# RWKV-5 attention and soft-MoE slots on one core: one key half moved to GpSimd's load queue, a three-row last weight piece, and a new order

## The chip, the core and the metric

The kernel runs on one core of a Trainium2 chip. A core has five engines that run side by side and meet through semaphores: TensorE (PE in the profile; its weight loads stand apart as PEld), VectorE (DVE), ScalarE (ACT), GpSimd (POOL) and SyncE (SP). Transfers between the chip's main memory and the on-chip memory run on sixteen DMA engines. They are issued from SP's, ScalarE's or GpSimd's queue; only GpSimd's can turn fp32 into bf16 on the way. The metric is the device time of one execution in microseconds (us).

## The reference

Two parts, one behind the other. First a linear attention over 768 steps, for 4 batches and 8 heads of width 48, with a decaying 48 by 48 state for each head; then a mixture of experts, in which 32 slots (8 experts of 4) take softmax-weighted means of all 3072 tokens, go through a two-layer network each, and are mixed back to the tokens.

```python
for t in range(S):
    kt, vt, rt = (k[:, :, t], v[:, :, t], r[:, :, t])
    cur = np.einsum('bhd,bhe->bhde', u[None] * kt, vt)
    y[:, :, t] = np.einsum('bhd,bhde->bhe', rt, state + cur)
    state = w[None, :, :, None] * state + np.einsum('bhd,bhe->bhde', kt, vt)
...
x = np.ascontiguousarray(attn_out.transpose(0, 2, 1, 3)).reshape(B * S, H * D)
logits = x @ phi
d = softmax over the tokens, c = softmax over the slots
slot_input = d.T @ x
h = np.maximum(slot_input[e] @ w1[e], 0.0)
slot_out[e] = h @ w2[e]
return c @ slot_out
```

All inputs and the output are fp32. k, r and v have 1.18 million elements each, phi is 384 by 32, w1 is 8 by 384 by 1024, w2 8 by 1024 by 384, the output 3072 by 384.

## The kernel before

**Loads.** The 768 steps are cut into six chunks of 128. Each chunk of k, r and v comes in two halves (two batches each, 192 KB as bf16): L0 and L1 are the halves of k for chunk 0, L2 and L3 those of r, L4 and L5 those of v, and so on up to L35. Behind them on the same queue come the eight w1 (W0 to W7, 768 KB each) and the eight w2 (V0 to V6, and expert 7 in two pieces, Va7 with its first rows and Vb7 with the last YL rows; a row is 1/8 of an expert's w2, 96 KB). All of these are issued by GpSimd, which converts them to bf16, except L0 and L1: these are loaded as fp32 into `k0`, a corner of the w1 buffer that is still free, L0 by SP and L1 by ScalarE (lines 253 and 254). phi and u are loaded by SP behind L0, w by ScalarE ahead of L1. GpSimd's issue waits until one of the last eight loads has landed, so that at most eight of its loads are in flight. w2 goes into the buffers of the chunks of k, r and v, so its issue also waits for the copies out of them (line 822).

**Set-up.** DVE clears and fills constants; GpSimd makes an index table and the identity, and clears the padding of the two rp buffers (line 267). `zt0` to `zt3` (DVE) and `ze0` to `ze3` (ACT) make the tables of decay factors, `za`, `zb`, `zd` the mask, the u column and phi in bf16. `fill(n)` issues n dummy products on PE.

**A chunk.** `q..` copies a loaded tensor with padding into an rp buffer (for chunk 0 of k in two halves, `qk00` and `qk01`); `t..` turns it with 16 transposes on PE (line 376), `e..` takes it out of PSUM on DVE or ACT, for k and r with the decay factors. `A` and `M` are the scores and their mask, `pr`, `D`, `ds` and `dv` the diagonal term, `b` and `kn`, `vn` the transposes back, `s` and `S` the state, `Y` and `x` the output of the attention, `X`, `xT`, `l` and `lg` the logits. `mx`, `sb`, `ex`, `c` and `cT` make the weights of the slots for the way back. After chunks 3, 5 and 6 a group (`gm` to `acc`) adds the tokens' share to the slots' inputs with a running maximum.

**The end.** `h` is the first expert layer (48 products), `hs` its relu, `ht` and `hT` its transpose. `o00` to `o70` are the second layer, expert by expert, eight rows each, in one PSUM bank SO. For expert 7 the work is cut: `o70` takes the rows of Va7, then `so1` copies the sum so far; `o7` with the remaining rows (`o76` for rows 6 and 7) completes it and `so2` copies that. The first four of the 24 output rows (128 tokens each) do not wait for so2: their product `p` uses so1, and the last weight rows are added from `gG`, a product of the hidden layer with cT that is made earlier, one for each of these rows (`pg`, line 795, YL products for each output row; row 0 is made in halves a and b). The other 20 use so2. `oe` takes a row out of PSUM, even rows on ACT, odd ones on DVE, and `dm` (SP) stores one, two, four or eight rows. The order around it is fixed by `turn_`: p0a, p0b, p1, pg0a, pg0b, pg1, the last o, p2, pg2, p3, pg3, p4.

**The order.** The order in which all of this is issued, on every engine, is written out by hand in the string `ORDER`. A token is a piece's name; the numbers behind the colon are its buffers, a letter behind a slash its engine (D, A or P). `WARM` lists dummy products `F0`, `F1`, ... on PE and the piece each batch stands behind: three behind o50, six behind o60, three behind o70.

Of the kernel before, what the change touches and what calls it, by code (L numbers as in the profile page):

```python
# [21 lines left out]
A000:0,0 pr00:0/D tk10:1,1 ev01:/A iL16 M000 tk11:2 pr01:/P kn00:/A bk01:3,1 bv00:4,0 ek10 A001:0,1 ek11 vn00:/A  # L22
bv01:5,1 iL17 qr1:0/D D0:0,0 qv1:1/A s00:1,2,0 M001 iL18 tr10:4,1 iL19 S101 ds0:/A vn01:/A A010:0,2 iL20 tr11:0
S100 iL21 bk10:2,2 er10 qk2:0/A bk11:5,0 iL22 er11 tv10:1,1 dv00:0 M010 tv11:4 kn10:/A qr2:1/A ev11:/D iL23
Y000:0,0 kn01:/D Y001:2 iL24 A011:0,0 iL25 s01:4,3,1 x000:/A M011 x001:/A tk20:0,0 iL26 ev10:/A X00:2,0 pr10:0/P
S111 A100:0,1 kn11:/A tk21:1 ek20 tr20:3,0 xT00:/A M100 bv10:5,2 qv2:0/A bv11:0,3 iL27 tr21:2 ek21 iL28 pr11:/D
bk20:1,1 iL29 vn10:/A er21 iL30 kn20:/A er20 s10:5,2,2 iL31 vn11:/A qk3:1/D tv20:1,0 iL32 S110 bk21:3,2 dv01:1 S200
D1:0,1 kn21:/A ev20:/D s11:4,5,3 S201 ds1:/A tv21:1 iL33 pr20:0/D Y011:3 iL34 ev21:/A Y010:0,1 S210 A101:0,0 iL35
pr21:/D l00:2 x010:/A bv20:4,0 iW0 M101 x011:/A D2:1,0 dv10:0 bv21:0,1 vn20:/A X01:3,1 lg00:/D ds2:/A A110:0,2 S211
# [76 lines left out]
def kernel(  # L106
# [13 lines left out]
    B, H, S, D = r.shape  # L120
# [34 lines left out]
    pe, dve, act, pool, sp = nc.tensor, nc.vector, nc.scalar, nc.gpsimd, nc.sync  # L155
# [12 lines left out]
    def raw_t(x):  # L168
        return raw[:, x * RAWN:(x + 1) * RAWN]
# [60 lines left out]
    def load_rkv(y):  # L230
        x, bb = divmod(y, 2)
        c, which = divmod(x, 3)
        src = (k, r, v)[which].rearrange("(bb bl) h (c p j) d -> c bb (bl h) p (j d)", bb=2, bl=2, p=RR, j=JJ)
        O(pool.dma_start(out=raw_t(x)[:, bb * JJ * D:(bb + 1) * JJ * D], in_=src[c, bb]))  # L234
# [8 lines left out]
    def fill(n):  # L243
        for _ in range(n):
            O(pe.matmul(pG[0][:], ones[:, 0:128], ones[:], start=True, stop=True))

    P.fill = fill
    k0 = early[:, 2560:2560 + 2 * JJ * D]


    k_src = k.rearrange("(bb bl) h (c p j) d -> c bb (bl h) p (j d)", bb=2, bl=2, p=RR, j=JJ)
    O(act.dma_start(out=w_r[:, :, 0:D], in_=w[:, None, :].to_broadcast([H, 2, D])))
    for bb, q in ((0, sp), (1, act)):
        O(q.dma_start(out=k0[:, bb * JJ * D:(bb + 1) * JJ * D], in_=k_src[0, bb]))
    O(act.preload_act_table_set("natural_log_exp_and_others"))
    O(dve.memset(ident_f[:], 0.0))
    for t in (w_r, u_r):
        O(dve.memset(t[:, :, D:], 1.0))
    O(dve.memset(ones[:], 1.0))
    O(sp.dma_start(out=phi_f[:], in_=moe_phi.rearrange("(p mo) s -> p mo s", mo=nM)))  # L260
    O(sp.dma_start(out=u_r[:, :, 0:D], in_=u[:, None, :].to_broadcast([H, 2, D])))
    O(pool.iota(it_i.rearrange("p (j y) -> p j y", j=JJ), pattern=[[-1, JJ], [-JJ, RR]], base=C - 1,
                channel_multiplier=0))
    O(pool.affine_select(out=ident_f[:], in_=ident_f[:], compare_op=ALU.not_equal, fill=1.0, base=0,
                         pattern=[[-1, 128]], channel_multiplier=1))
    for t in rp_r:
        O(pool.memset(t[:, :, :, D:], 0.0))
# [85 lines left out]
    def turn(c, which):  # L353
# [506 lines left out]
```

## Time and profile before

| | |
|---|---|
| time, median of 3 runs | 117.49 us (117.24 to 117.93) |
| time of the profiled execution | 117.38 us |
| its span, first to last instruction | 115.6 us |
| PE busy | 98.7 us, 85% |
| PE weight loads | 76.0 us, 66% |
| DVE busy | 89.8 us, 78% |
| ACT busy | 76.7 us, 66% |
| POOL busy | 66.4 us, 57% |
| GpSimd's DMA queue (q0) | 19.27 MB, 85.7% of the sixteen engines' span |
| SP's DMA queue (q1) | 5.16 MB, 11.8% |
| ScalarE's DMA queue (q10) | 0.40 MB, 1.4% |
| read and written in main memory | 39.38 MB, 4.72 MB |

A row of the timeline or of a group reads: start, time, engine, line of the kernel, operation, what is written and read, shape, count, and in brackets how long the engine stood idle before and for whom. A row "DMA to landing" is the time from the start of an issue to the last of its sixteen completions. A row of the chain of waits is start, time, engine, what is written and the line. A row of a table by stretch is the stretch, its length, the busy time of PE, PEld, DVE, ACT and POOL with counts, the granted clock, the DMA engines' share and GB/s. A row of a DMA queue in a stretch is its number and kind, packets, MB, and the time its packets took as a share of sixteen engines; packets overlap, so that this can pass 100%.

### The profile page before, as it was taken

How to read it: one execution, taken by the hardware profiler on the slowest of the kernel's cores; microseconds unless marked ns; L12 is line 12 of the kernel's file. 1: busy time of each engine (PE TensorE's matmuls, PEld its weight loads, DVE VectorE, ACT ScalarE, POOL GpSimd, SP SyncE). 2: the span in 40 equal slices, each digit the busy share in tenths (PEclk: the TensorE clock that was granted, in tenths of full speed). 3: DMA queues.
4: the chain of work that ended last, by engine and by line, in shares of the span. 5: the costliest groups of instructions: out<-in, count | busy, mean ns of one | idle time of the engine just before them, and what ended most of it. 6: DMA issues, size and time to landing. Idle time of an engine off the chain costs nothing.

```text
span 115.6 us, 3911 instructions
## 1 busy us (share of the span) xinstructions
PE 98.7 (85%) x1649; PEld 76.0 (66%) x1649; DVE 89.8 (78%) x178; ACT 76.7 (66%) x124; POOL 66.4 (57%) x85
## 2 busy tenths in 40 slices
PE   4906999989899999999989999999999999999000
PEld 0306998869788889888868898888664653453000
DVE  6745979999999989999999999999883730379400
ACT  2947088999879797979996662898853440189100
POOL 7925589999699998069999999656030000000000
PEclk9999999999999999999999999999999999999965
DMA  2999999999999999999999999999999997059994
GB/s 36 268 197 206 207 205 210 205 206 208 208 210 201 229 219 208 218 219 212 210 220 215 210 220 210 214 219 212 215 223 208 217 209 149 17 208 404 408 438 174
DMA packets 9137, 25.08 MB, mean 217 GB/s; under 512 B 1184, under 2 KB 6176, under 8 KB 8992
## 3 DMA queue, kind: packets, MB, share of 16 engines
q0 software_dynamic: 7344, 19.27, 85.7%
q1 hardware_dynamic: 1608, 5.16, 11.8%
q10 hardware_dynamic: 168, 0.40, 1.4%
q8 instruction: 13, 0.21, 0.7%
q14 instruction: 4, 0.03, 0.1%
HBM read 39.38 MB, written 4.72 MB: 381 GB/s over the span
## 4 chain that ended last, share of the span: by engine, by line
PE 48%; DMA 17%; DVE 11%; ACT 9%; POOL 5%; issue 3%; DVEq 0%; ACTq 0%; POOLq 0%
DMA w_all<-in_moe_w_dram 17%; PE pG L376 9%; PE pA L415 4%; PE pG L788 3%; ACT rp L222 3%; PE pG L397 3%; PE pA L826 3%; PE pG L743 3%; PE pG L633 2%; PE pG L716 2%; PE pG L516 2%; PE pG L551 2%; POOL w_all L237 2%; PE pG L490 2%; PE pG L496 2%
## 5 line engine op out<-in xcount | busy, mean ns | idle before, releaser
L421 DVE TENSOR_TENSOR AT<-pA,mask 128x1024 bf16<-128x1024 f32 x24 | 29.2, 1218 | 1.3 <-PE pA L415 1.1
L376 PE MATMUL pG<-ident,rp 128*128 128x128 bf16 x288 | 22.5, 235 | 2.6 <-DVE rp L224 2.4
L376 PEld LDWEIGHTS <-rp 128*128 128x128 bf16 x288 | 19.2, 106 | 3.8 <-issue 2.8
L428 POOL TENSOR_TENSOR pr<-kT,rT 128x1024 bf16<-128x1024 bf16 x8 | 17.0, 2130 | 5.1 <-DVE rT L386 4.6
L445 POOL TENSOR_TENSOR dv<-vn,ds 128x768 bf16<-128x768 bf16 x12 | 17.7, 1482 | 3.0 <-DVE sd L540 2.2
L222 ACT COPY rp<-raw 128x1536 bf16<-128x1536 bf16 x11 | 16.3, 1479 | 2.6 <-PE pG L376 2.3
L222 ACT COPY vT<-pG 128x1024 bf16<-128x1024 bf16 x8 | 8.0, 1015 | 5.2 <-PE pG L376 5.2
L474 DVE TENSOR_TENSOR S<-pG,W 128x384 bf16<-128x384 f32 x20 | 10.5, 548 | 0.5 <-PE pG L466 0.5
L803 ACT ACTIVATE w_all<-pG,rcs 128x384 f32<-128x384 f32 (+1 forms) x12 | 5.8, 587 | 6.1 <-PE pG L795 5.9
L415 PE MATMUL pA<-rT,kT 64*128 64x128 bf16 x192 | 9.5, 218 | 0.3 <-DVE AT L421 0.2
L386 DVE TENSOR_TENSOR kT<-pG,Tk 128x1024 bf16<-128x1024 bf16 x12 | 8.0, 684 | 1.7 <-PE pG L376 1.3
L222 ACT CAST x<-pG 128x384 bf16<-128x384 f32 x19 | 8.5, 487 | 0.8 <-PE pG L498 0.5
L222 ACT COPY xT<-pG 128x768 bf16<-128x768 bf16 x10 | 8.0, 804 | 1.3 <-PE pG L516 1.2
L496 PE MATMUL pG<-vn,AT 128*128 128x48 bf16 x192 | 8.7, 183 | 0.2 <-ACT kn L222 0.2
L222 ACT COPY vn<-pG 128x768 bf16<-128x768 bf16 x10 | 8.0, 815 | 0.9 <-PE pG L397 0.9
L805 DVE TENSOR_SCALAR w_all<-pG,rcs 128x384 f32<-128x384 f32 (+1 forms) x13 | 6.9, 596 | 1.6 <-PE pG L795 1.6
L234 POOL DMA_DIRECT2D raw<-in_v_dram x12 | 6.3, 537 | 3.1 <-DMA raw<-in_r_dram 3.0
L386 DVE TENSOR_TENSOR rT<-pG,Tr 128x1024 bf16<-128x1024 bf16 x12 | 7.9, 683 | 0.0
L498 PE MATMUL pG<-dv,ident 128*128 128x384 bf16 x24 | 7.7, 323 | 0.0
L222 ACT COPY kn<-pG 128x768 bf16<-128x768 bf16 x9 | 7.3, 812 | 0.5 <-PE pG L397 0.5
L415 PEld LDWEIGHTS <-kT 64*128 64x128 bf16 x192 | 5.7, 94 | 2.8 <-issue 1.1
L496 PEld LDWEIGHTS <-AT 128*128 128x128 bf16 x192 | 7.1, 96 | 0.4 <-issue 0.4
(139 smaller groups left out, 216.2 us busy)
## 6 DMA issues: line engine op xcount, KB each, us to landing
w_all<-in_moe_w_dram POOLq DMA_DIRECT2D x8, 768.0 KB, 18.8
raw<-in_moe_w_dram POOLq DMA_DIRECT2D x7, 768.0 KB, 25.5
raw<-in_r_dram POOLq DMA_DIRECT2D x12, 192.0 KB, 7.2
raw<-in_v_dram POOLq DMA_DIRECT2D x12, 192.0 KB, 6.8
raw<-in_k_dram POOLq DMA_DIRECT2D x10, 192.0 KB, 7.2
out_dram<-w_all SPq DMA_DIRECT2D x2, 768.0 KB, 3.8
out_dram<-w_all SPq DMA_DIRECT2D x1, 1536.0 KB, 6.1
out_dram<-w_all SPq DMA_DIRECT2D x4, 192.0 KB, 2.0
```

The source lines that it names most:

```text
L222: O(act.copy(dst, src))
L234: O(pool.dma_start(out=raw_t(x)[:, bb * JJ * D:(bb + 1) * JJ * D], in_=src[c, bb]))
L376: O(pe.transpose(o[:, :, j, :], rp_r[W[rp]][:, jh * JH + j].rearrange("p b d -> p (b d)"), ident[:]))
L386: O(dve.tensor_mul(dst, src, (Tk, Tr)[which][:, None, jh].to_broadcast(BC)))
L415: O(pe.matmul(pA[:, bb, h4 * C:(h4 + 1) * C], kt[s, bl, h].rearrange("p a x -> p (a x)"), rt[s, bl, h].rearrange("p a x -> p (a x)"), star ...
L421: O(dve.tensor_mul(AT_r[W[f"AT{key}"]][:], pA[:].rearrange("p bb (h t) -> p bb h t", t=C), mask[:, None, None, :].to_broadcast([128, 2, H ...
L428: O(op(e).tensor_mul(pr_r[W[f"pr{c}"]][:, bl], kT_r[W[f"kT{c}"]][:, bl].rearrange("p h j x -> p h (j x)"), rT_r[W[f"rT{c}"]][:, bl].rearra ...
L445: O(op(e).tensor_mul(dv_r[W[f"dv{c}{bl}"]][:], vn_r[W[f"vn{c}{bl}"]][:], ds_r[W[f"ds{c}"]][:, bl, :, :, None].to_broadcast([128, H, 2, D])))
L474: O(dve.tensor_mul(S_r[W[new]][:, s], bank(kb[hf])[:, 0:HD].rearrange("p (h b d) -> p h b d", b=2, d=D), W128[:, s, :, None].to_broadcast( ...
L496: O(pe.matmul(o[:, z:z + D], AT_r[W[at]][:, bb, h4, :], vn[:, hf * H2 + h4, bb, :], start=(c == 0 and h4 == 0 and bb == 0), stop=False, sk ...
L498: O(pe.matmul(o[:, 0:HD], ident[:], dv_r[W[f"dv{c}{bl}"]][:, hf * H2:(hf + 1) * H2] .rearrange("p h b d -> p (h b d)"), start=False, stop= ...
L805: O(dve.tensor_scalar(out=dst, in0=src, scalar1=rcs[:, i:i + 1], scalar2=None, op0=ALU.mult))
```

## The change

- L1 is no longer loaded as fp32 by ScalarE. It is GpSimd's first load, into the buffer of k's chunk 0, ahead of L2 to L5. `qk01` reads it from there. The limit of eight loads in flight now counts it (the first wait stands at the tenth load of the list instead of the eleventh), and expert 0's w2, which overwrites it, waits for qk01.
- phi is loaded by ScalarE, behind w; u is the second load of SP.
- The padding of the rp buffers is cleared by DVE, behind the three first dummy products in the program, instead of by GpSimd ahead of its first load.
- YL is 3 instead of 2: Va7 has five rows, Vb7 three; o70 has five products, the last o (now `o75`) three; there is a third gG product with its copy; each pg has three products. All gG stand ahead of o40.
- WARM: one dummy behind o50, five behind o60, two behind o70, instead of three, six, three.
- ORDER is written anew from first to last. The pieces and their dependences are otherwise the same; the places, the buffers and part of the engines are others. `qk00` is on DVE and `qk01` on ACT (before: the other way round), the pr pieces are 7 on DVE and 5 on GpSimd (before: 4 and 8).

```diff
-WARM = [("gl1", 2), ("gb2", 3), ("dp2", 2), ("o50", 3), ("o60", 6), ("o70", 3)]
+WARM = [("gl1", 2), ("gb2", 3), ("dp2", 2), ("o50", 1), ("o60", 5), ("o70", 2)]
...
-zt3 zc iL6 zt1 ze3 iL7 zw:0 zt0 ze1 iL8 zb ze0 iL9 zt2 qk00:0/A za zd:/D ze2 qk01:/D iL10 tk00:0,0 tk01:1 qr0:1/A
-iL11 ek00 iL12 ek01 tr00:2,0 qv0:0/D iL13 tr01:3 er00 iL14 tv00:4,0 er01 tv01:5 ev00:/A iL15 bk00:0,0 qk1:1/D
...
-hs10:/A h00:1 hs11:/D h01:4 hs00:/D ht1:0 hs01:/A c5:3 hT1:/D ht0:2 cT5:/A gG0:5 hT0:/D rs:1 gE0:/A gG1:4 rr o00:0
-gE1:/A o10 o20 o30 o40 o50 F7 F8 F9 o60 F10 F11 F12 F13 F14 F15 o70 F16 F17 F18 so1 p0a:3 p0b:2 p1:5 pg0a pg0b pg1
-oe0a oe0b o76 p2:1 oe1 dm00 pg2 so2:/A p3:4 dm01 pg3 oe2 p4:3 p5:2 oe3 p6:5 dm02 oe4 p7:0 p8:1 oe5 oe6 p9:4 dm03
...
+zt0 zc iL6 za ze0 iL7 zt1 iL8 qk00:0/D ze1 zt2 qk01:/A iL9 zt3 ze2 zw:0 tk00:0,0 iL10 zb ze3 tk01:1 qr0:1/D iL11
+ek00 tr00:2,0 iL12 ek01 tr01:3 qv0:0/A iL13 er00 bk00:4,0 er01 iL14 bk01:5,1 pr00:0/D kn00:/A tv00:0,0 iL15
...
+rs:5 rw h01:0 rr h00:1 hs01:/D h10:4 hs00:/A h11:2 hs10:/A ht0:3 hs11:/A hT0:/D ht1:5 gG1:0 hT1:/D o00:1 o10 gE1:/D
+o20 o30 gG0:4 gG2:2 o40 gE0:/A gE2:/D o50 F7 o60 F8 F9 F10 F11 F12 o70 F13 so1 F14 p0a:3 p0b:5 p1:0 pg0a pg0b pg1
+oe0a oe0b o75 dm00 oe1 p2:4 pg2 so2:/A dm01 p3:2 pg3 oe2 p4:3 p5:5 dm02 oe3 p6:0 oe4 p7:1 p8:4 oe5 oe6 p9:2 dm03
...
-    k0 = early[:, 2560:2560 + 2 * JJ * D]
+    k0 = early[:, 2560:2560 + JJ * D]
...
-    for bb, q in ((0, sp), (1, act)):
-        O(q.dma_start(out=k0[:, bb * JJ * D:(bb + 1) * JJ * D], in_=k_src[0, bb]))
+    O(sp.dma_start(out=k0, in_=k_src[0, 0]))
+    O(act.dma_start(out=phi_f[:], in_=moe_phi.rearrange("(p mo) s -> p mo s", mo=nM)))
...
-    O(sp.dma_start(out=phi_f[:], in_=moe_phi.rearrange("(p mo) s -> p mo s", mo=nM)))
...
+    for x in range(1, 6):
+        load_rkv(x)
+    fill(3)
     for t in rp_r:
-        O(pool.memset(t[:, :, :, D:], 0.0))
-    load_rkv(2)
-    load_rkv(3)
-    load_rkv(4)
-    load_rkv(5)
-    fill(3)
+        O(dve.memset(t[:, :, :, D:], 0.0))
...
-    YL = 2
+    YL = 3
...
-            P.add("i" + name, "POOL", lambda e, f=fns[kind], x=x: f(x), deps=[lands[n - 8]] if n >= 10 else [])
+            P.add("i" + name, "POOL", lambda e, f=fns[kind], x=x: f(x), deps=[lands[n - 8]] if n >= 9 else [])
...
-                    e, rp_r[W[rp]][:, :, bb, 0:D], k0[:, bb * JJ * D:(bb + 1) * JJ * D].rearrange("p (j d) -> p j d", j=JJ)),
+                    e, rp_r[W[rp]][:, :, bb, 0:D], (raw_t(0)[:, JJ * D:2 * JJ * D] if bb else k0).rearrange("p (j d) -> p j d", j=JJ)),
...
+    P.by["o40"]["deps"] += [f"gG{y}" for y in range(YL)]
...
-            P.by[f"i{kind}{e}"]["deps"] += [f"q{'krv'[x % 3]}{x // 3}" for x in (2 * e, 2 * e + 1) if x]
+            P.by[f"i{kind}{e}"]["deps"] += [f"q{'krv'[x % 3]}{x // 3}" for x in (2 * e, 2 * e + 1) if x] + ([] if e else ["qk01"])
```

More of the change, by code (lines that the diff above doesn't have):

```diff
@@ L25 @@
[L25 to L29, printed above, removed]
@@ new lines @@
+ek00 tr00:2,0 iL12 ek01 tr01:3 qv0:0/A iL13 er00 bk00:4,0 er01 iL14 bk01:5,1 pr00:0/D kn00:/A tv00:0,0 iL15
+A000:0,0 kn01:/D zd:/A pr01:/P qk1:1/A tv01:1 M000 ev01:/A tk10:2,1 qr1:0/D iL16 A001:0,1 tk11:3 ev00:/A ek10 iL17
+tr10:4,1 M001 iL18 qv1:1/A tr11:5 bv00:1,0 iL19 D0:2,0 er10 iL20 A010:0,2 vn00:/A bv01:0,1 er11 iL21 tv10:4,1
+ds0:/D vn01:/A ek11 dv00:0 tv11:1 s00:5,2,0 M010 ev10:/A s01:3,0,1 iL22 ev11:/A pr10:0/D Y000:4,0 iL23 S111
+A011:0,0 x000:/A bv10:1,2 iL24 pr11:/D Y001:0 iL25 M011 vn10:/A bv11:4,3 dv01:1 x001:/A D1:1,1 vn11:/A S100
@@ new lines @@
+A100:0,1 X00:0,0 S101 ds1:/A iL26 bk10:5,2 S110 xT00:/A Y010:4,1 iL27 M100 Y011:1 kn10:/A iL28 bk11:2,0 l00:3
+x011:/A qk2:0/D iL29 s10:0,5,2 qr2:1/A x010:/D dv10:0 A101:0,2 S200 tk20:1,0 M101 tk21:4 kn11:/A X01:0,1 iL30
+qv2:0/A Y100:2,2 iL31 S201 A110:0,0 ek20 iL32 Y101:5 M110 x100:/A iL33 tv20:1,0 xT01:/A dv11:1 tv21:2 x101:/A ek21
+A111:0,1 l01:0 ev21:/A X10:5,0 M111 iL34 xT10:/A s11:4,2,3 iL35 lg01:/D qk3:0/D lg00:/A iW0 Y111:0 ev20:/A mx0 S211
+tk30:5,1 iW1 sb0:0/D tk31:3 S210 ex0:0 bv20:2,0 iW2 ek30 qr3:0/A bv21:1,1 ek31 c0:4 tr20:5,0 iW3 cT0:/D tr21:3
@@ new lines @@
+vn20:/A er20 Y110:4,3 iW4 er21 vn21:/A bk20:5,1 tr30:2,1 iW5 qv3:1/D x111:/A A200:0,2 pr20:0/D x110:/A tv30:3,1 iW6
+M200 tv31:1 ev30:/A X11:0,1 iW7 l10:4 pr21:/D A201:0,1 xT11:/A tr31:3 kn20:/D lg10:/A qk4:1/A M201 D2:0,0 s20:5,4,0
+ds2:/D A210:0,0 S300 qr4:0/A dv20:0 l11:0 er30 bk21:5,2 er31 bk30:2,0 lg11:/A dv21:1 ev31:/A M210 Y201:0 Y200:3,4
+kn30:/A S301 bv30:1,2 x200:/A A211:0,1 x201:/D iV0 Y210:2,5 vn30:/A pr30:0/D zu tk40:4,0 M211 x210:/A X20:3,0
+tk41:0 xT20:/A bv31:1,3 mx1 pr31:/D A300:0,2 qv4:1/A Y211:2 ek41 D3:3,1 sb1:1/D l20:0 M300 iV1 x211:/A lg20:/A
@@ new lines @@
+vn31:/A tv40:2,0 ek40 tv41:0 ds3:/A ev40:/A X21:1,1 dv30:0 kn21:/D A301:0,0 ev41:/D tr40:3,0 xT21:/A M301 tr41:4
+dv31:1 qk5:1/A s21:5,2,1 er40 bv40:0,0 bv41:1,1 qr5:0/A er41 iV2 A310:0,1 S311 s30:3,4,2 pr40:0/P M310 vn41:/A
+Y300:2,6 vn40:/A S401 l21:1 A311:0,2 x300:/D lg21:/A bk31:4,1 ex1:1 pr41:/P S400 bk40:0,2 kn31:/A gm0 c1:1 bk41:2,0
+cT1:/A M311 tk50:3,1 kn41:/A gt0:4 tk51:1 iV3 kn40:/A gr00 D4:2,0 ek50 Y311:4 ds4:/A qv5:1/A S310 Y301:0 mx2
+A400:0,2 ek51 sb2:0/P Y310:2,7 dv40:0 M400 gd0 ex2:0 tv50:3,1 tv51:5 x311:/A x310:/A x301:/D gb0:1 A401:0,0 iV4
@@ new lines @@
+ev50:/A c2:4 gx0 gs0:/P M401 tr50:2,1 tr51:0 cT2:/A s31:1,3,3 dv41:1 ev51:/A er50 A410:0,1 er51 s40:4,2,0 ge0 S411
+pr50:0/P Y401:5 M410 dp0:0 S410 A411:0,0 S501 iV5 acc0 pr51:/P S500 bv50:3,2 M411 Y400:1,0 vn50:/A Y410:2,1 x401:/A
+x400:/D s41:0,4,1 x410:/A A500:0,2 iV6 S511 Y411:3 M500 D5:5,1 X30:1,0 x411:/A X31:2,1 ds5:/A xT30:/A bv51:4,3
+dv50:0 S510 A501:0,1 xT31:/D vn51:/A l30:3 M501 l31:5 X40:0,0 iVa7 lg31:/A X41:1,1 dv51:1 lg30:/D xT40:/A mx3
+A510:0,0 Y500:2,2 M510 xT41:/A l40:4 Y501:5 sb3:1/P x500:/A l41:3 lg40:/D ex3:1 A511:0,2 Y510:0,3 iVb7 x501:/A M511
```

29 lines of the change are left out of this document (5 added, 24 removed).

## Prediction

> **What bounds the kernel now.** I read the page's slices first, for where the load stream starts and stops.
>
> ```profile
> DMA  2999999999999999999999999999999997059994
> GB/s 36 268 197 206 207 205 210 205 206 208 208 210 201 229 219 208 218 219 212 210 220 215 210 220 210 214 219 212 215 223 208 217 209 149 17 208 404 408 438 174
> ```
>
> A slice is 2.9 us. From the second slice to the 33rd the sixteen DMA engines are never free and move the same 205 to 220 GB/s, so inputs and weights come as one unbroken stream; then there is a hole of two slices, then output. So I asked which instructions end the hole: the weight loads of line 240, one at a time (w2 of expert 6, the first six rows of expert 7, called Va7, its last two rows, Vb7), and the chain of waits at the end.
>
> ```profile
> L240 POOL DMA_DIRECT2D raw<-in_moe_w_dram x1: 593/593/593, 73.7 to 73.7; - x1
> ...
> DMA to landing us min/median/max: 25.0/25.0/25.0
> ...
> L240 POOL DMA_DIRECT2D raw<-in_moe_w_dram x1: 593/593/593, 71.0 to 71.0; - x1
> ...
> DMA to landing us min/median/max: 25.0/25.0/25.0
> ...
> L240 POOL DMA_DIRECT2D raw<-in_moe_w_dram x1: 593/593/593, 79.3 to 79.3; - x1
> ...
> DMA to landing us min/median/max: 20.3/20.3/20.3
> ```
>
> ```profile
> 96.12 0.75 PE pA L826 x3
> 96.88 0.44 PE pG L743 x8
> 97.32 1.40 PE pA L826 x6
> 98.75 0.50 PE pG L743 x6
> ...
> 100.38 0.66 PE pG L795 x6
> 101.04 0.27 PE pG L743 x2
> 101.31 0.27 PE pG L788
> 101.58 0.33 PE pG L795 x2
> 101.90 0.16 PE pG L788
> 102.06 0.33 PE pG L795 x2
> ```
>
> Issue plus time to landing gives expert 6 at 96.0, Va7 at 98.7, Vb7 at 99.6. The chain names only PE, but the products of line 826 are dummies: nine of them, 2.15 us, stand ahead of the six rows of o70, and o70 begins at 98.75, just behind Va7's 98.7. So the stream decides here, and PE has 2.15 us in hand. Everything after hangs on that moment: so1 (the copy of the sum so far), the products p and pg for output rows 0 to 3 with the last weight rows, and the output.
>
> ```profile
> 99.28 0.56 DVE L224 CAST vT<-pG 128x384 bf16<-128x384 f32 x1 [5.19 <-PE pG L743]
> ...
> 102.50 5.87 DVE L805 TENSOR_SCALAR w_all<-pG,rcs 128x384 f32<-128x384 f32 x11 [0.73 <-PE pG L795]
> ```
>
> ```profile
> 103.72 0.33 SPq L811 DMA_DIRECT2D out_dram<-w_all  x1
> ```
>
> ```profile
> 102.00:104.00 2.00, 1.96 (x12) 0.97 (x10) 1.50 (x3) 1.93 (x5) 0.00 (x0) 1.00 0.83 296
> ...
> 106.00:110.00 4.00, 0.84 (x4) 0.19 (x2) 2.37 (x5) 1.42 (x3) 0.00 (x0) 1.00 1.03 419
> 110.00:114.00 4.00, 0.00 (x0) 0.00 (x0) 0.00 (x0) 0.00 (x0) 0.00 (x0) 0.56 1.00 422
> ```
>
> The last two numbers of a stretch are DMA share and GB/s. Output starts thin (296 GB/s) and then runs at 420 to its end: at 0.47 us for a row of 192 KB (0.197 MB / 0.42), the 20 rows from the 103.72 issue on fill the time to 114 with under 1 us over. So output is bound by its own rate once row 4 is issued, and row 4 hangs on DVE's row of evictions, which starts at 102.50 behind pg3. A step that moves pg3 moves the end by as much; one that moves only rows 0 and 1 does not.
>
> **The change part by part.** Three things touch that path: when the stream lands, how it is cut at the end, and what stands between o70 and pg3.
>
> *The start of the stream.* Key half L1 leaves ScalarE's queue and becomes GpSimd's first load, ahead of L2; GpSimd loses the two memsets of rp.
>
> ```profile
> 0.74 0.66 SPq L254 DMA_DIRECT2D w_all<-in_k_dram  x1
> ...
> 1.33 0.98 POOL L267 MEMSET rp<- 128x512 bf16 x2
> 1.38 0.62 ACTq L254 DMA_DIRECT2D w_all<-in_k_dram  x1
> ...
> 2.26 1.25 POOL L234 DMA_DIRECT2D raw<-in_r_dram  x2
> ```
>
> ```profile
> q10 hardware_dynamic: 36, 0.11, 88.7%
> ...
> q0 software_dynamic: 12, 0.02, 20.2%
> ...
> q0 software_dynamic: 44, 0.07, 81.9%
> ...
> q0 software_dynamic: 61, 0.09, 103.9%
> ...
> q0 software_dynamic: 69, 0.10, 111.7%
> ...
> q0 software_dynamic: 148, 0.20, 114.6%
> ...
> q0 software_dynamic: 150, 0.20, 115.2%
> ```
>
> These are queues by stretch: q10 (ScalarE's) from 4.5 to 5, then q0 (GpSimd's) in four half microseconds from 5 to 7 and in 7:8 and 8:9. GpSimd's first issue begins at 2.26 and its first packets come between 5.0 and 5.5, with none before: about 3 us. By 9.0 it has sent 484 packets; at 150 a microsecond that is 3.23 us of work, as if it had started at full rate at 5.77. A load is 128 data packets and 16 semaphore writes, 144, so 0.96 us. With the memsets gone its first issue moves from 2.26 to 1.33: 0.93 earlier. With the same delay and the same slow start, L2 and all behind it move by -0.93 + 0.96 = +0.03: what GpSimd gains in the start, the extra load takes. The lower end: the slow start came from the other queue (q10 had 88.7% just before), which is gone; then L1 runs at full rate from 4.3 and L2 from 5.26, -0.5. The upper end: the first packets do not come earlier at all, and L2 waits one load more, +0.96. The row is nearest to the first; I take -0.15, since part of the contention does go.
>
> The Trainium skill, page "DMA: Bandwidth & Descriptors", section "Latency and other measured facts", gives about 1 us to the first byte on GpSimd's path and 0.6 on the hardware path. By that figure (an estimate from the page) L1 would start near 2.3, the engines would have no gap, and the time would be near 116. The 3 us of this trace speak against it, and the sum goes by the trace.
>
> *The cut at the end.* From Va7's landing to Vb7's are 0.97 us for two rows, from expert 6's to Va7's 2.7 for six: 0.45 to 0.48 a row. With five rows Va7 lands 0.47 earlier; Vb7's landing stays. o70 is five products instead of six (0.50; two cost 0.27), -0.05. So so1 and the first p move by -0.52, to 99.3 and 99.7 for pg0a, just behind Vb7's 99.6.
>
> *Between o70 and pg3.* Each pg has three products instead of two: the piece of six (0.66) becomes nine (0.99), and the two pairs (0.33) become triples (0.50): +0.33 + 0.17 + 0.17 = +0.67. The last o has three rows instead of two, +0.04 (eight cost 0.44, two 0.27). So pg3 moves by -0.52 + 0.71 = +0.19. Bounds: 0, if the rows ahead of pg3, which gain, carry the output; +0.4, if pg0a comes to wait for Vb7 and PE loses its run.
>
> *What is hidden.* PE gets its first real work earlier:
>
> ```profile
> 8.70 0.52 POOL L234 DMA_DIRECT2D raw<-in_v_dram  x1 [2.08 <-DMA raw<-in_r_dram]
> ...
> 9.78 5.28 PE L376 MATMUL pG<-ident,rp 128*128 128x128 bf16 x48 [2.43 <-DVE rp L224]
> ```
>
> L2 had landed at 8.65 (GpSimd's wait for it ends there); L1 in its place, 0.93 earlier, lands near 7.7, and with a 0.8 us copy on ScalarE the transposes start near 8.6 instead of 9.78. That is 1.2 us for PE, worth nothing at the end as long as the stream decides, and 1.2 if PE did. The extra gG product and its copy, 0.4 to 1 us, and the removal of three dummies ahead of o70 (0.75 us) draw on the same 2.15 us in hand. The third fewer dummy stands beside so1's 0.56 us on DVE: nothing. The rp memsets on DVE cost it up to 0.98 there, before tables that nothing needs until L1 has landed. u moves up in SP's queue, phi to ScalarE's; neither is needed before the 15th microsecond. GpSimd's load window moves with the extra load (eight in flight, as before). No wait is new on GpSimd except expert 0's w2 on the copy of L1, 35 us after that copy.
>
> *Sum.* -0.15 + 0.19 = +0.04. The profiled execution took 117.38 us (115.6 of span and 1.8 around it), 0.1 under the median of 117.49. So 117.42, told as 117.4.
>
> **The rivals.**
> 1. *The stream starts a good deal sooner*: no slow start and no idle engine ahead of it. Then -0.5 to -0.93 for the stream and +0.19 at the end: 116.6 to 117.1, taken as 116.8. For it: GpSimd is free at 1.33 and q10's traffic is gone. Against: 3 us from issue to packets.
> 2. *The stream starts no sooner* (the other side): the first packets come near 5.2 whatever the issue time, since something other than the issue holds them, and L1 is a load in front of all others. Price +0.96 less up to 0.25 for the second half's packets that no longer compete, +0.19 at the end: 118.3. It decides from first packets later than about 4.9. For it: the trace shows one start only, so delay and fixed time cannot be told apart. Against: packets of the other queues filled the engines until then.
> 3. *PE comes late to o70.* All of the order between is written anew, and PE is busy through the middle; if it loses more than the 1.2 us gained and the 1 us or so of the hand that is left, the dummies no longer stand in a gap. One microsecond past that point costs one: 118.5. For it: five dummies still stand between o60 and o70. Against: PE's idle time was small already, so a new order starts from the same total.
> 4. *PE runs slow at the end.* The 48 transposes at 9.78, after an idle stretch, took 0.110 us each; sixteen later ones the half:
>
> ```profile
> 21.63 1.06 PE L376 MATMUL pG<-ident,rp 128*128 128x128 bf16 x16
> ```
>
> With fewer dummies PE may stand idle for about 1 us before o60 and half a microsecond before o70; were that enough, the 3 us of products from o70 to pg3 would take up to twice that: about 119.5. The Trainium skill, page "TensorE: Matmul & The Clock Gate", section "Part 1: The HAM clock gate (the "warmup" mystery)", puts the fall to half rate after an idle window of some 3.4 us; by that rule these gaps are too short. No row of this trace shows a shorter gap do it.
>
> **How the numbers follow.** Forecast 0.46, at 117.4, own range 116.9 to 118.0. Rival 1 0.22, rival 2 0.14, rival 3 0.13, rival 4 0.05. A measurement of this kernel tells about 0.5% from no change, 0.6 us either side of 117.49, so 116.9 to 118.1 is "same": that is the forecast, 0.46. Faster is rival 1, 0.22; slower are rivals 2 to 4, 0.32. The range holds the forecast, nearly all of rival 1 and most of rivals 2 and 3: 116.6 to 118.6, with the ends that the stream's start (-0.5 to +0.96) and the tail (0 to +0.4) make.
>
> **What would show it.** Right: q0's first packets near 4.3; loads that land within 0.3 us of where they did; Va7 half a microsecond before its old place, with o70 right behind it; pg3 about 0.2 us later than 102.39 against Vb7's landing; DVE's row of evictions and the output moved by the same. Wrong: a landing of Vb7 that moved by more than half a microsecond (rivals 1 and 2); o70 well behind Va7's landing (rival 3); products of 384 columns over 0.2 us apart in the tail (rival 4); or output that no longer runs at 420 GB/s from row 4 on.

## The result and the profile after

The changed kernel takes 118.17 us (median of 14 runs, 117.52 to 118.57); the kernel before, on the same chip, 117.50 us (14 runs). The ratio is 1.0048 with a 95% interval of 1.0027 to 1.0069: slower by about half a per cent, where 117.4 us and no measurable change were forecast. The profiled execution took 117.92 us with a span of 116.1 us; the one of before 117.38 and 115.6. So the profiles differ by 0.54 us, and it can be looked for in them. One execution, the profiled one of e1 below, took 295.24 us; it is not counted in that run's median, and its profile is not read.

The slices first: the load stream is as it was up to the 33rd. The slices around the hole and the last one differ (76 GB/s at a share of 1 at the end, where before had 174 at 4), but the two spans are cut into 40 parts each, so that towards the end the edges lie up to half a microsecond apart.

```profile
DMA  2999999999999999999999999999999995079991
GB/s 28 236 200 206 207 213 202 205 209 205 209 206 213 218 218 216 212 221 210 214 222 207 217 220 207 218 219 214 212 215 217 216 203 103 7 276 412 415 449 76
```

Next the chain of waits of after, from Va7's issue to the end of pg3 (line 792 is the old 795, 785 the old 788, 740 the old 743).

```profile
74.44 23.62 DMA raw<-in_moe_w_dram
98.07 0.04 issue
98.11 0.50 PE pG L740 x5
...
98.63 0.57 DVE vT L224
...
99.25 0.49 PE pG L785 x3
99.73 0.98 PE pG L792 x9
100.72 0.27 PE pG L740 x3
100.99 0.27 PE pG L785
101.26 0.49 PE pG L792 x3
101.75 0.16 PE pG L785
101.91 0.49 PE pG L792 x3
102.39 1.19 PE pG L785 x7
```

Va7 lands at 98.07 instead of 98.7, o70 starts 0.04 us behind it, and pg3, now with three products (the pieces of line 792 take 0.98, 0.49 and 0.49), ends at 102.39: to the hundredth where it ended before. The timeline says the same of the engines around it: PE stood idle for the landing ahead of o60 and o70, the products there are 0.06 to 0.1 us apart, and DVE's row of evictions, from which row 4 and all others are stored, begins at 102.43 instead of 102.50.

```profile
95.80 0.51 PE L740 MATMUL pG<-raw,rT 128*32 128x384 bf16 x8 [1.09 <-DMA raw<-in_moe_w_dram]
...
98.11 0.49 PE L740 MATMUL pG<-raw,rT 128*32 128x384 bf16 x5 [0.62 <-DMA raw<-in_moe_w_dram]
...
102.43 5.87 DVE L802 TENSOR_SCALAR w_all<-pG,rcs 128x384 f32<-128x384 f32 x11 [1.06 <-PE pG L792]
```

By the prediction's own reading the end should then be where it was. It isn't. These are the queues between 102 and 115, after first and before second, with the row of SP's last store: its size and the time from issue to landing.

```profile
DMA packets 1232, 4.63 MB, mean 356 GB/s; under 512 B 144, under 2 KB 591, under 8 KB 1103
## 3 DMA queue, kind: packets, MB, share of 16 engines
q1 hardware_dynamic: 1231, 4.62, 88.9%
q14 instruction: 1, 0.01, 0.1%
...
out_dram<-w_all SPq DMA_DIRECT2D x1, 1536.0 KB, 6.7
```

```profile
q1 hardware_dynamic: 1296, 4.72, 91.0%
...
out_dram<-w_all SPq DMA_DIRECT2D x1, 1536.0 KB, 6.1
```

The last store, eight rows, is issued at 108.4 in both kernels and takes 6.7 us instead of 6.1. And after has a row that before does not have: one packet on q14, a queue of instruction fetches. (The number of packets on q1 cannot be compared; some records are missing in after.) The stretches at the end show how the delay looks:

```profile
113.50:114.00 0.50, 0.00 (x0) 0.00 (x0) 0.00 (x0) 0.00 (x0) 0.00 (x0) 0.50 0.93 393
114.00:114.50 0.50, 0.00 (x0) 0.00 (x0) 0.00 (x0) 0.00 (x0) 0.00 (x0) 0.50 0.07 25
```

```profile
113.50:114.00 0.50, 0.00 (x0) 0.00 (x0) 0.00 (x0) 0.00 (x0) 0.00 (x0) 0.50 0.93 393
114.00:114.50 0.50, 0.00 (x0) 0.00 (x0) 0.00 (x0) 0.00 (x0) 0.00 (x0) 0.50 0.02 0
```

After first. Up to 114.0 the two are alike, 393 GB/s. Then before is done, and after moves 25 GB/s for another half microsecond: 393 / 25 is 16, so one of sixteen engines is still writing (a share of 0.07 of sixteen engines over 0.5 us is 0.56 us of one). The sixteen completions that the traces hold for the last store say the same. Before has all of them between 114.41 and 114.56. After has fifteen between 114.32 and 114.48, and the sixteenth at 115.05. A store is done when the last engine is. A narrow stretch of after finds the fetch:

```profile
q1 hardware_dynamic: 16, 0.09, 110.0%
q14 instruction: 1, 0.01, 9.7%
```

This is 108.6 to 108.8, in the middle of the output: 9.7% of sixteen engines over 0.2 us is 0.31 us of one engine. In the kernel before the trace has a q14 packet too, but at 116.1, when the output is out. Its row in that microsecond:

```profile
q14 instruction: 1, 0.01, 2.0%
```

What moved it can be guessed from the busy time and instructions of each engine; before first, then after. Only ScalarE's (ACT) went up by several instructions, from 124 to 129:

```profile
PE 98.7 (85%) x1649; PEld 76.0 (66%) x1649; DVE 89.8 (78%) x178; ACT 76.7 (66%) x124; POOL 66.4 (57%) x85
```

```profile
PE 98.5 (85%) x1648; PEld 75.3 (65%) x1651; DVE 90.9 (78%) x176; ACT 80.0 (69%) x129; POOL 60.9 (52%) x84
```

From this came the theory of the experiments (in the expectations F, or the theory of the instruction fetch): the rewritten order puts a few more pieces on ScalarE; its instructions are fetched in blocks, so its next block is asked for a few instructions earlier in its program; that point now lies in the saturated output, where the fetch delays one of sixteen engines, and the final store waits for it. The rivals: the order itself, the three rows, or the new start.

### The profile page after: what moved, and what is told of

It is laid out like the page before. It is cut to its first block, busy times and chain, and to the rows that moved or that the text cites. A ratio compares the mean times of both kernels' runs of the same rounds, so it can differ in the third digit from the quotient of the medians.

```text
span 116.1 us, 3894 instructions
## 1 busy us (share of the span) xinstructions
PE 98.5 (85%) x1648; PEld 75.3 (65%) x1651; DVE 90.9 (78%) x176; ACT 80.0 (69%) x129; POOL 60.9 (52%) x84
## 4 chain that ended last, share of the span: by engine, by line
PE 35%; DMA 32%; POOL 12%; ACT 6%; issue 4%; DVE 3%; DVEq 0%; POOLq 0%; ACTq 0%
DMA raw<-in_moe_w_dram 20%; PE pG L373 7%; DMA raw<-in_k_dram 6%; POOL raw L234 6%; DMA raw<-in_v_dram 5%; PE pG L394 4%; POOL dv L442 4%; PE pA L412 3%; PE pG L785 3%; ACT rp L222 3%; PE pG L487 3%; PE pG L493 2%; PE pG L495 2%; DVE w_all L802 2%; POOL pr L425 2%
## 5 line engine op out<-in xcount | busy, mean ns | idle before, releaser
L373 PE MATMUL pG<-ident,rp 128*128 128x128 bf16 x288 | 21.2, 228 | 2.1 <-ACT rp L222 1.9
L373 PEld LDWEIGHTS <-rp 128*128 128x128 bf16 x288 | 18.2, 102 | 4.0 <-ACT rp L222 2.3
L222 ACT COPY rp<-raw 128x1536 bf16<-128x1536 bf16 (+1 forms) x13 | 18.4, 1437 | 2.2 <-DMA raw<-in_v_dram 2.2
L222 ACT COPY vn<-pG 128x768 bf16<-128x768 bf16 x12 | 9.5, 818 | 3.9 <-PE pG L394 3.9
L222 ACT COPY vT<-pG 128x1024 bf16<-128x1024 bf16 x11 | 11.0, 1024 | 1.1 <-PE pG L373 1.1
L425 POOL TENSOR_TENSOR pr<-kT,rT 128x1024 bf16<-128x1024 bf16 x5 | 10.6, 2130 | 0.3 <-DVE rT L383 0.2
L234 POOL DMA_DIRECT2D raw<-in_r_dram x12 | 6.6, 554 | 1.7 <-DMA raw<-in_k_dram 1.7
```

The lines of the kernel that those rows point to most:

```text
L222: O(act.copy(dst, src))
L373: O(pe.transpose(o[:, :, j, :], rp_r[W[rp]][:, jh * JH + j].rearrange("p b d -> p (b d)"), ident[:]))
L425: O(op(e).tensor_mul(pr_r[W[f"pr{c}"]][:, bl], kT_r[W[f"kT{c}"]][:, bl].rearrange("p h j x -> p h (j x)"), rT_r[W[f"rT{c}"]][:, bl].rearra ...
```

## The experiments

Each run stands against the kernel before, timed on the same chip. ScalarE's instructions are given twice: as the page counts them, and with the records that it leaves out (issues, waits of the sequencer), as some expectations count them. "Fetch" is where the last q14 packet lies ("behind the output" means that it comes after the last completion of the last store); "last store" is the time from issue to landing of the eight rows. The runs were timed on three chips (e1 to e4, e5 to e8, e9 to e11), on which the kernel before has medians of 117.55, 117.56 and 117.44 us; between chips the ratios are the better measure. All the medians here come from 12 runs, 14 for the first two and 11 for e1.

| run | ScalarE, page / all | fetch, us | last store, us | median, us | ratio [95%] |
|---|---|---|---|---|---|
| before | 124 / 192 | behind the output | 6.1 | 117.50 | |
| after | 129 / 195 | 108.7 | 6.7 | 118.17 | 1.0048 [1.0027, 1.0069] |
| e1_after_again | 129 / 195 | - | - | 117.91 | 1.0027 [0.9994, 1.0059] |
| e2_after_less_act | 124 / 189 | behind the output | 6.2 | 117.33 | 0.9975 [0.9945, 1.0005] |
| e3_before_more_act | 132 / 200 | 107.5 | 6.8 | 118.25 | 1.0055 [1.0022, 1.0088] |
| e4_after_two_rows | 129 / 195 | 108.4 | 6.7 | 117.91 | 1.0019 [0.9990, 1.0048] |
| e5_before_one_act | 125 / 193 | behind the output | 6.3 | 117.68 | 1.0005 [0.9981, 1.0029] |
| e6_scalar_key_half | 124 / 189 | behind the output | 6.1 | 117.35 | 0.9974 [0.9953, 0.9996] |
| e7_less_act_two_rows | 124 / 189 | behind the output | 6.3 | 117.58 | 0.9989 [0.9959, 1.0019] |
| e8_after_more_act | 151 / 217 | 97.0 | 6.1 | 117.69 | 1.0002 [0.9970, 1.0034] |
| e9_tail_alone | 124 / 192 | behind the output | 6.1 | 117.62 | 1.0004 [0.9982, 1.0026] |
| e10_two_tokens | 127 / 192 | behind the output | 6.1 | 117.51 | 0.9991 [0.9965, 1.0016] |
| e11_start_alone | 124 / 192 | behind the output | 6.3 | 117.26 | 0.9985 [0.9960, 1.0011] |

**The changed kernel again**, unaltered.

> The changed kernel unaltered, for a second profile. What is to be explained: in its first profile Va7 lands about 0.6 us earlier than before, pg3 and DVE's row of evictions start where they did, yet the last store lands 0.5 us later, on one of the sixteen DMA engines only. Theory F (an instruction fetch of ScalarE or another engine, queue q14, now falls into the output stream at 108.7 and holds up one DMA engine): the fetch stands there again and the store ends 0.5 us after the other fifteen. Theory T (the three-row tail is what costs): pg3 stands later than 102.4 in this profile. Theory S (the load stream lands at another time in most executions): Va7 lands at 98.5 or later. All three: 117.9 to 118.3 us.

Measured 1.0027 and 117.91 us; the interval reaches from no change past the first result.

**Fewer instructions on ScalarE.** Five steps of the gate (small copies, lg) go to VectorE, all between 30 and 90 us; nothing else.

Shown is the line of lg10; lg11, lg20, lg21 and lg31 lose their A for a D in the same way.

```diff
-M200 tv31:1 ev30:/A X11:0,1 iW7 l10:4 pr21:/D A201:0,1 xT11:/A tr31:3 kn20:/D lg10:/A qk4:1/A M201 D2:0,0 s20:5,4,0
+M200 tv31:1 ev30:/A X11:0,1 iW7 l10:4 pr21:/D A201:0,1 xT11:/A tr31:3 kn20:/D lg10:/D qk4:1/A M201 D2:0,0 s20:5,4,0
```

> The changed kernel with five small copies of logits (lg10, lg11, lg20, lg21, lg31) moved from ScalarE to DVE, so that ScalarE's program is five instructions shorter and its next fetch of instructions comes after the end, as in the kernel before. Theory F: no q14 packet between 102 and 114 us, the last store lands with the others, 0.5 us faster than the changed kernel, 117.5 to 117.7. Theories T and S: DVE has 1 us more to do in the middle, which the loads hide; the time stays at 118.1 (within 0.2).

117.33 us, 0.58 under e1's median and a little below the 117.5 to 117.7 of the expectation. The table of queues of e2 between 102 and 115 has no row of q14, and the last store takes 6.2 us. This agrees with the theory, but the moved steps change the order too.

**More instructions, or only more work, on ScalarE, in the kernel before.** e3 adds eight copies of one column near the end of the set-up; e5 adds a single copy of 1792 columns at the same place. Neither result is read by anything.

e3, then e5; not shown are the piece's place in ORDER, behind qr0, and the place that it writes to.

```diff
+    P.add("na", "ACT", lambda e: [O(act.copy(nap[:], ident_f[:, 0:1])) for _ in range(8)])
```

```diff
+    P.add("na", "ACT", lambda e: O(act.copy(nap, ident_f[:, None, :].to_broadcast([128, 14, 128]))))
```

> The kernel before with eight one-column copies on ScalarE, in its idle stretch between 11 and 14 us; nothing else is changed. Theory F: ScalarE's fetch now comes before the end, inside the output stream, and one DMA engine ends late: 0.3 to 0.6 us slower, 117.8 to 118.1. Theories T and S: nothing changes, 117.5 (within 0.2).

> The kernel before with one long copy on ScalarE (1792 columns, about 1.7 us) where e3 had eight short ones: the same time on ScalarE at the same place, but one instruction instead of eight. Theory F (it is the count of ScalarE's instructions, which brings its fetch into the output stream): no q14 packet between 102 and 114 us, 117.5, within 0.2 of the kernel before. Rival P (in e3 it was the 1.75 us of ScalarE at the start that cost): as e3, 118.1 to 118.4.

The timeline of each has the same load on ScalarE, 1.75 and 1.68 us at the same moment:

```profile
10.84 1.75 ACT L346 COPY nap<-ident_f 128x1 f32<-128x1 f32 x8
```

```profile
10.64 1.68 ACT L346 COPY w_all<-ident_f 128x1792 f32<-128x1792 f32 x1
```

Eight instructions cost half a per cent (1.0055, its interval above 1.002; the 118.25 us are a little over the 117.8 to 118.1 of the expectation), one with the same busy time costs nothing that can be told (1.0005). e3 has the packet in the queues between 102 and 115, and its last stretches show the same picture of one engine:

```profile
q14 instruction: 1, 0.01, 0.1%
...
out_dram<-w_all SPq DMA_DIRECT2D x1, 1536.0 KB, 6.8
```

```profile
114.00:114.50 0.50, 0.00 (x0) 0.00 (x0) 0.00 (x0) 0.00 (x0) 0.00 (x0) 0.50 0.93 393
114.50:115.00 0.50, 0.00 (x0) 0.00 (x0) 0.00 (x0) 0.00 (x0) 0.00 (x0) 0.50 0.07 25
```

Its sixteenth completion comes at 115.71, 0.45 us behind the fifteenth; in e5 the two are 0.04 apart. The profiled execution of e5 took 118.50 us all the same: its Va7 landed only at 99.52. So one profile's total says little, and the distance of the last completion from the others is the surer sign. The delay can be made in the kernel before, without the new order, the three rows or the new start, and it follows the number of instructions, not ScalarE's time.

**Still more instructions, in the changed kernel.** 22 such copies behind gE0.

```diff
-o20 o30 gG0:4 gG2:2 o40 gE0:/A gE2:/D o50 F7 o60 F8 F9 F10 F11 F12 o70 F13 so1 F14 p0a:3 p0b:5 p1:0 pg0a pg0b pg1
+o20 o30 gG0:4 gG2:2 o40 gE0:/A na gE2:/D o50 F7 o60 F8 F9 F10 F11 F12 o70 F13 so1 F14 p0a:3 p0b:5 p1:0 pg0a pg0b pg1
...
+    P.add("na", "ACT", lambda e: [O(act.copy(nap[:], ident_f[:, 0:1])) for _ in range(22)])
```

> The changed kernel with 22 one-column copies added on ScalarE behind gE0, in its idle stretch from 94.4 to 100 us, so that its fetch comes there, ahead of the output stream, where the load stream ends. Theory F: the q14 packet stands between 95 and 101, none between 102 and 114, the last store lands with the others, and the kernel is 0.3 to 0.6 us faster with more work in it: 117.4 to 117.7. Rival (the fetch is a bystander): 118.0 or more.

More work on ScalarE (83.8 us busy instead of 80.0) and no slower: the fetch has moved ahead of the output, into the stretch from 96.8 to 97.2, and the store takes 6.1 again, with its sixteen completions within 0.2 us. By the times alone (1.0002 with an interval that overlaps e1's) this would not be settled; the store's time is what shows it. The 22 copies follow one another without a gap across the fetch: they take 4.87 us, 0.22 each, as in e3.

```profile
q14 instruction: 1, 0.01, 5.0%
```

**Only two of the five steps moved**, to tell the count from the order: the edit of lg10 as shown for e2, and this one.

```diff
-ds2:/D A210:0,0 S300 qr4:0/A dv20:0 l11:0 er30 bk21:5,2 er31 bk30:2,0 lg11:/A dv21:1 ev31:/A M210 Y201:0 Y200:3,4
+ds2:/D A210:0,0 S300 qr4:0/A dv20:0 l11:0 er30 bk21:5,2 er31 bk30:2,0 lg11:/D dv21:1 ev31:/A M210 Y201:0 Y200:3,4
```

> The changed kernel with only two instructions of the order moved from ScalarE to VectorE (the gate's steps lg10 and lg11), so that ScalarE has some 193 recorded instructions, one more than before and two fewer than the changed kernel. Theory of the instruction fetch: no row of queue q14 between 102 and 114 us, the last store lands within 0.1 us of the slowest of the other engines, and the time is that of the version with five steps moved: ratio 0.996 to 0.999, 117.1 to 117.5 us. Rival, that the order itself (which work of the gate lies on ScalarE ahead of the weights) made the difference: 2 of 5 steps bring 0.25 us of the 0.66, so 117.7 to 117.9 us, ratio 1.001 to 1.003, with the fetch wherever it likes.

0.9991 and 117.51 us are a hair over the upper ends that the theory gave (0.999 and 117.5) and under the rival's 1.001 and 117.7. The interval lies wholly under that of after, but it reaches 1.0016, so the time alone does not exclude the rival; the store's 6.1 us and the packet's place behind the output are what speak against it. ScalarE's records are 192, not the 193 that were counted ahead.

Over all versions: the three profiles with the fetch inside the output (after, e3, e4) have the sixteenth completion of the last store 0.45 to 0.58 us behind the fifteenth, the nine without it 0.01 to 0.04. The four ratios of kernels with the fetch there (e1 counted as after) are 1.0019 to 1.0055, the eight of the others 0.9974 to 1.0005.

**Two rows instead of three in the changed kernel**, with the fetch (e4) and, on top of e2, without it (e7).

```diff
-    YL = 3
+    YL = 2
...
```

In ORDER the third gG with its copy goes, and the last o is `o76` again.

> The changed kernel with YL back at 2: six and two weight rows for expert 7, two gG products, two products for each pg; order and dummies otherwise as in the changed kernel. Theory T (three rows cost more than the earlier Va7 brings): 0.2 to 0.6 us faster than the changed kernel. Theories F and S, and the prediction's sum for this step (+0.19 for three rows): within 0.2 us of the changed kernel, at most 0.2 faster; Va7 lands 0.47 us later than with five rows and pg3 comes 0.2 us earlier after it.

> e2 with YL back at 2 (as e4, but without the fetch in the output stream). By the prediction's sum, three rows cost +0.19, so 0.1 to 0.2 faster than e2: 117.1 to 117.3; from o70's start to pg3's end 3.7 us instead of 4.3, and Va7 0.47 us later. If the cut at the end is worth its half microsecond: 0.3 slower, 117.6.

e4 has e1's median, 117.91. e7's is 0.25 us over e2's, on another chip (ratios 0.9989 and 0.9975, with intervals that overlap); it lies at the 117.6 of the expectation's second case and not at the 117.1 to 117.3 of the first. Neither is a difference that can be told from none, so no gain or loss of the cut at the end is shown. That Va7 lands 0.47 later with six rows is not seen in single profiles: 0.20 later in e4 than in after, 1.67 later in e7 than in e2. The chain of e4 gives the price of the row: o70 to the end of pg3 from 98.31 to 102.02, 3.71 us, where after has 98.11 to 102.39, 4.28 us. e4 against e7 is the fetch once more: 6.7 against 6.3 us for the store, ratios of 1.0019 and 0.9989, whose intervals overlap.

```profile
98.31 0.52 PE pG L740 x6
...
101.69 0.33 PE pG L792 x2
102.02 1.26 PE pG L785 x7
```

**L1 back on ScalarE's queue as fp32**, on top of e2, phi back to SP; the rp memsets stay on VectorE.

```diff
-    O(sp.dma_start(out=k0, in_=k_src[0, 0]))
-    O(act.dma_start(out=phi_f[:], in_=moe_phi.rearrange("(p mo) s -> p mo s", mo=nM)))
+    for bb, q in ((0, sp), (1, act)):
+        O(q.dma_start(out=k0[:, bb * JJ * D:(bb + 1) * JJ * D], in_=k_src[0, bb]))
...
```

> e2 with the start's transfers as before: L1 as fp32 by ScalarE, phi by SP behind L0; the rp memsets stay on DVE, so GpSimd's first load is L2, near 1.46 us. Its length against e2 is one instruction either way on SP and GpSimd, none on ScalarE. If the engines' work is what counts (L1 costs the same on either queue and there is no gap): Va7 lands within 0.2 us of e2's, 117.2 to 117.5. If L1 ahead of L2 on GpSimd's queue costs its 0.96 us there: up to 0.5 faster than e2, 116.8 to 117.0. If the ScalarE queue's half slows the start as it did before: 0.2 to 0.3 slower, 117.6.

The ratio is 0.9974 against e2's 0.9975: the route of L1 cannot be seen in the time. Va7 was to land within 0.2 us of e2's and landed 0.46 later (98.13 against 97.67), no more than single profiles of one start differ by.

**The start alone and the tail alone, in the kernel before.** e11 has the loads, memsets and window of the changed kernel, with the order and the tail of before:

```diff
-    for bb, q in ((0, sp), (1, act)):
-        O(q.dma_start(out=k0[:, bb * JJ * D:(bb + 1) * JJ * D], in_=k_src[0, bb]))
+    O(sp.dma_start(out=k0, in_=k_src[0, 0]))
+    O(act.dma_start(out=phi_f[:], in_=moe_phi.rearrange("(p mo) s -> p mo s", mo=nM)))
...
+    for x in range(1, 6):
+        load_rkv(x)
...
```

e9 has the three rows with their products and the fewer dummies, with the start and the order of before otherwise:

```diff
-WARM = [("gl1", 2), ("gb2", 3), ("dp2", 2), ("o50", 3), ("o60", 6), ("o70", 3)]
+WARM = [("gl1", 2), ("gb2", 3), ("dp2", 2), ("o50", 1), ("o60", 5), ("o70", 2)]
...
-    YL = 2
+    YL = 3
```

> The kernel before with the edits at the start alone: the second key half as GpSimd's first load, phi as second on ScalarE's queue, the rp memsets on VectorE, the window of the first products moved; order and tail as before. ScalarE's instruction count is that of before, so no row of q14 in the output stream. The prediction's first term: -0.15 us (bounds -0.5 and +0.96), so 117.4 us, ratio 0.9987; with the same delay of the first row and a slow start of GpSimd's queue +0.03 us, ratio 1.0002. The rival that the stream starts later: +0.5 to +0.9 us, ratio over 1.004.

> The kernel before with the tail alone: the last piece of Va holds three rows, with its products and the gate's tail pairs, and fewer dummy products; loads at the start as before. ScalarE's instruction count is at most that of before, so no row of q14 in the output stream. The prediction's sum of these terms (Va7 with five rows -0.47, o70 -0.05, pg3 later +0.71): +0.19 us, 117.7 us, ratio 1.0016. By the profiles of the versions with three rows and no fetch (end 17.45 to 17.59 us behind Va7's landing where two rows had 16.9 to 17.2): -0.1 to +0.2 us, ratio 0.999 to 1.002. If the three rows themselves were what made the changed kernel slower: +0.5 to +0.7 us, ratio over 1.004.

Both agree with the sum as far as they can be told: 117.26 is 0.18 us under the kernel before on the same chip (117.44; forecast -0.15), and e9 is 0.18 over it by the medians and 0.05 by the ratio (forecast +0.19). Neither interval excludes zero; what they exclude is half a per cent from either part alone. For e9 the agreement has another cause in it: PE comes late there, and five dummies hold o70 until 98.65, about 0.35 us behind Va7's landing at 74.0 + 24.3 = 98.3; from there to the end of pg3 it takes 4.23 us. The load and the chain:

```profile
L240 POOL DMA_DIRECT2D raw<-in_moe_w_dram x1: 591/591/591, 74.0 to 74.0; - x1
...
DMA to landing us min/median/max: 24.3/24.3/24.3
```

```profile
97.47 1.19 PE pA L826 x5
98.65 0.44 PE pG L743 x5
...
102.39 0.49 PE pG L795 x3
102.88 1.26 PE pG L788 x7
```

## Why the prediction was wrong, point by point

**The step that failed** is in the reading of the bound: "output is bound by its own rate once row 4 is issued", with the conclusion that only a step that moves pg3 moves the end. The output is bound by the slowest of sixteen engines, and something that isn't output can lie in that engine's way. pg3 did not move (102.39 in both), DVE's row started 0.07 us earlier, and the end came half a microsecond later. The new order entered the prediction only as a danger for PE (rival 3); that it gives ScalarE three more recorded instructions, and that instructions too come through the DMA engines, had no term. The missing term is about +0.5 us: 6.7 to 6.8 us for the last store in the three profiles with the fetch inside the output, 6.1 to 6.3 us in the nine without. With it the sum is 0.04 + 0.5, and the profiles differ by 0.54. That it fits so closely is luck: pg3 moved by 0.00 and not by 0.04, the last completion by 0.49, and the other 0.05 lie behind it.

The Trainium skill, page "Runtime: NRT & Kernel Launch", section "Instruction fetch mechanics", says that each engine's sequencer has a DMA queue of its own with which it fetches the next block of instructions, and that the cost of crossing into a block is "mostly hidden". That fetches are DMA transfers is what the rows of q14 show; the pages of the profile list two such queues, q8 and q14, so that each engine has its own is not shown here. The second holds here for the engine that fetches: in e8 no wait of ScalarE for it is seen. It does not hold for the stream that the fetch crosses, where it cost 0.5 us.

**The start** was right in its direction and too small in its size. GpSimd's first issue begins at 1.46 (1.33 forecast). This is its row, and these are q0's rows in the half microseconds from 3.5 to 5:

```profile
1.46 0.70 POOL L234 DMA_DIRECT2D raw<-in_k_dram  x1
```

```profile
q0 software_dynamic: 7, 0.01, 11.8%
...
q0 software_dynamic: 44, 0.07, 79.0%
...
q0 software_dynamic: 71, 0.10, 116.1%
```

The first packets come between 3.5 and 4, so 2.0 to 2.5 us behind the issue instead of about 3, ahead of the 4.3 that was named. The slow start is still there, at 79% only in the second of these stretches. In the first and second of them SP's and ScalarE's queues are at work too (71.6% and 25.0%, then 16.8% and 27.3%). From 0 to 9 us q0 moves 484 packets and 0.67 MB in before, 688 packets and 0.95 MB in after, which is 0.28 MB more. L1 is 0.20 of it, so the rest of the stream leads by 0.08 MB, 0.4 us at 0.20 MB a microsecond, where the sum had 0.15. The lead lasts: from 0 to 80 us it is 15.84 MB against 15.56, the same 0.28. With the same start, e2, e8, e10 and e11 (0.94, 0.93, 0.91 and 0.93 MB by 9 us) lead by 0.2 to 0.35 us. Rival 2 (first packets near 5.2) is out. Rival 1 is nearer than it was given: the packets were early, but the lead is 0.4 us and not 0.5 to 0.93, and e11's gain in time is 0.18 us, with an interval that includes no change.

**The cut at the end** agrees to a few hundredths, with luck in both terms. Va7 was to land 0.62 earlier (0.15 of the start, 0.47 of the row) and landed 0.63 earlier in this profile, though the start gave more than its 0.15. Among the profiles with five rows in Va7 and the same loads the landing ranges from 97.67 (e2) to 98.53 (e10), so one profile does not carry a tenth.

```profile
74.45 23.22 DMA raw<-in_moe_w_dram
97.67 0.04 issue
```

```profile
74.31 24.22 DMA raw<-in_moe_w_dram
98.53 0.04 issue
```

From o70 to the end of pg3 was to become 0.66 longer (0.71 - 0.05) and became 4.28 - 3.64 = 0.64 longer. The pg products did as forecast (+0.64 for +0.67), but o70 and the last o take what they took before (0.50 and 0.27), and two terms that the sum put at nothing cancel. With a dummy less behind o70 the first p begins 1.14 us behind o70's start instead of 1.25, and the first three p products take 0.49 us instead of 0.38.

**PE** (rivals 3 and 4): it stands idle for 1.09 us ahead of o60 and 0.62 us ahead of o70, with the landing as releaser, so the new order did not make it late; and the products behind these gaps are as fast as before where the same are compared: nine of line 792 in 0.98 us and three in 0.49, where before six took 0.66 and two 0.33. (Rival 4 read the sixteen later transposes as half of 0.110 us each; they took 1.06 / 16 = 0.066.) Both rivals are out, and with them the 0.18 of chance that was put on "slower" for a reason of PE. The time came out within the range for a reason that none of the four named.

## What to carry to other kernels

Where a kernel ends in a store that saturates the DMA engines, look into the last stretch for anything that is not the store, and compare the time from issue to landing of the last store: here one foreign packet on one engine delayed the whole store. A rewritten order changes the number of instructions on an engine and so the place of its instruction fetches; when two versions differ by half a per cent without a wait to show for it, see where these packets fall before blaming the edit. Here two small steps moved to another engine took the loss away: the change with these two moved gives 0.9991. With five steps moved it gives 0.9975, and with the old route for L1 besides 0.9974 [0.9953, 0.9996]: these two versions lie furthest under the kernel before, by a quarter of a per cent, and only for the second does the interval leave out no change.

## What the runs showed of the hardware

An instruction fetch of ScalarE delays the last store by 0.45 to 0.58 us where it falls inside the output (after, e3, e4). Where it falls at the end of the loads (e8) or behind the output, no delay of the store is seen; whether it costs the loads something was not measured. The packet itself occupies 0.31 us of one engine (9.7% of sixteen engines over 0.2 us), yet the engine ends about 0.56 us late in after; what makes up the rest was not tried.

Where the fetch falls goes by the count of instructions in steps: with 193 records of ScalarE and fewer it lay behind the output, with 195 and 200 inside it (108.7, 108.4, 107.5), with 217 at 97.0. The count of records alone does not give the place: 192 of the 195 records had begun before the packet in after, 197 of the 200 in e3 and 184 of the 217 in e8. The other queue of instruction fetches, q8, has 13 packets of 16 KB (0.21 MB) in every page of this kernel and was not varied; whether one of them can be moved out of the first output row's way stays open.
